# Attention values of a head pair on the two column halves of TensorE, with the softmax sums taken by VectorE

## The chip, the cores and the metric

The kernel runs on one core of one Trainium2 chip. The metric is the device time of one execution in microseconds (us), lower is better. The engines are named as in the profile: PE (TensorE matmul), PEld (its weight loads), DVE (VectorE), ACT (ScalarE), POOL (GpSimd) and SP (SyncE, here the DMA queue).

## The reference

```python
batch, n_heads, seq_l, seq_g, head_dim = (8, 8, 512, 32, 64)
...
s_g = scale * np.matmul(q_g, k_all.transpose(0, 1, 3, 2))
out_g = np.matmul(sm(s_g), v_all)          # 32 global queries see all 544 keys
...
mask = np.abs(pos[:, None] - pos[None, :]) <= 32
s_ll = np.where(mask, s_ll, -1000000000.0) # 512 local queries see a band
s_l = np.concatenate([s_lg, s_ll], axis=-1) # and the 32 global keys
out_l = np.matmul(sm(s_l), np.concatenate([v_g, v_l], axis=2))
...
x = attn_out.transpose(0, 2, 1, 3).reshape(B * S, H * D)
h = x @ w_in                               # 512 -> 2048
g = np.maximum(h, 0.0) + np.log1p(np.exp(-np.abs(h)))
out = g @ w_out                            # 2048 -> 512
```

`sm` subtracts the row's maximum, takes the exponential and divides by the sum plus 1e-9. All data is fp32.

## The kernel before

The work has two parts. Attention runs on pairs of heads: pair m holds two heads, 64 rows of the partitions each, and batch b has the pairs 4b to 4b + 3. The dense layers (the MoE of the code) run per batch in a block of 16 tiles f of 128 hidden columns: 12 passes `h` (input, in a high and a low fp32r half against a weight in two halves) and later 12 passes `o` per f. Blocks 0 to 7 treat the local tokens of one batch, a half block at the end the global tokens of all. In block 0 the weights are also loaded and split into halves, four DVE operations for each of 32 pieces. Batch 0's attention (pairs 0 to 3) runs ahead of everything in code of its own. All other pairs go through `pieces`: small pieces of work with a due number, 12 numbers to a pair, slipped in between the passes of the MoE blocks, which emit the pieces as their own progress `at` moves from `first + 48 * b` to `first + 48 * (b + 1)`; block 0 goes from START = 69 to first + 48.

Each pair is cut into three pieces p of up to 288 queries; a piece has two chunks of 128 keys (32 global keys and 96 local ones). `scores(m, p)` makes scores with keys on the partitions, both heads at once on the two halves of the array's rows (64 rows each), into the PSUM tile "a". For pairs below 8 the mask is added by PE, and ACT copies the scores out; from 8 on DVE adds the mask (L315). L316 is a DVE operation that transposes blocks of 32 x 32 and takes the maximum along the keys, into `mt`. `maxima` folds these partial maxima over the four partition groups (three POOL copies, then short DVE reductions) and spreads them; `probs` spreads them over the keys by a DVE transpose (L347, into `mb`), subtracts on POOL (L352 to L355) and takes the exponential on ACT.

`values(m, p)` multiplies with v. The stationary operand has 65 columns: 64 of v and a column of ones, so that row 64 of the result is the softmax sum. Each head writes its own bank of the PSUM tile "a", partitions 0 to 64. ACT copies the result into `x`, and DVE adds the columns where neighbouring pieces overlap (L374, L375). "a" exists once (two banks), and scores and values share it: every user waits until the one before has been read. `combine`, `invert` and `normalise` take the sums through DRAM: row 64 is written out, read back as 38 x 32, gets 1e-9 and a reciprocal, is written back and read again spread over 64 partitions (`rb`), and two DVE products make the normalised `xa`, head 0 on partitions 0 to 63 and head 1 on 64 to 127. `split_x` makes the fp32r halves `xh` (ACT) and `xl` (DVE) of it for the next block. The 32 global queries stand in all three pieces; the overlap additions sum them too.

PE's order is the order of the code (`mm` chains each matmul to the one before). On the other engines a scheduler sets the order, apart from the dependencies that `after` adds.

Of the kernel before, what the change touches and what calls it, by code (L numbers as in the profile page):

```python
# [53 lines left out]
def moe_over_global_local_attention(  # L54
# [271 lines left out]
    def maxima(m):  # L326
        mt = st.pop(("mt", m))
        for a in range(1, 4):
            nc.gpsimd.tensor_copy(mt[0:32, GW * a:GW * a + GW], mt[32 * a:32 * a + 32, 0:GW])
        e0 = 4 * GW  # L330
        for u, du, off in ((0, 1, -2), (3, 1, 3)):
            nc.vector.tensor_reduce(grid(mt, e0 + u, (7, 6), (du, 2)), grid(mt, 3 + u, (12, 6), (du, 2), (off, 2), (GW, 4)), axis=AX.XY, op=ALU.max)
        nc.vector.tensor_reduce(grid(mt, e0 + 2, (7, 6), (4, 2)), grid(mt, 3 + 2, (12, 6), (7, 2), (GW, 4)), axis=AX.X, op=ALU.max)
# [1 line left out]
        nc.vector.tensor_reduce(grid(mt, g, (1, 2)), grid(mt, 3 + 5, (36, 2), (12, 3), (3, 2), (GW, 4)), axis=AX.XYZ, op=ALU.max)
        nc.vector.tensor_copy(grid(mt, e0 + 5, (21, 2), (7, 3)), mt[0:32, g:g + 2].unsqueeze(2).to_broadcast([32, 2, 3]))
# [6 lines left out]
    def probs(m, p):  # L343
# [12 lines left out]
        nc.scalar.activation(s, s, AF.Exp, scale=0.125)  # L356

    def values(m, p):
        s, vt = st.pop(("s", m, p)), st["v", m]
# [13 lines left out]
        nc.scalar.copy(x[:, :, o + 64:o + w], ps[0:65, :, 64:w])
        nc.vector.tensor_tensor(x[:, :, o:o + 64], x[:, :, o:o + 64], ps[0:65, :, 0:64], op=ALU.add)  # L374
        nc.vector.tensor_tensor(x[:, :, 160:192], x[:, :, 160:192], ps[0:65, :, 160:192], op=ALU.add)  # L375
# [5 lines left out]
    def combine(m):
        nc.sync.dma_start(out=rec_dram[2 * m:2 * m + 2], in_=st["x", m][64:65])

        rows = rec_dram[2 * m:2 * m + 2].rearrange("h (s k) -> (h s) k", k=32)
        sc = pl.tile([38, 32], F32, tag="sc", name=f"sc{m}", bufs=1)
        nc.sync.dma_start(out=sc, in_=rows)
        st["sc", m] = sc, rows

    def invert(m):
# [9 lines left out]
    def normalise(m):  # L399
# [3 lines left out]
        for h in range(2):  # L403
            after(nc.vector.tensor_tensor(y[64 * h:64 * h + 64], x[0:64, h], rb[:, h], op=ALU.mult), "scores")  # L404
# [341 lines left out]
```

## Time and profile before

| | |
|---|---|
| time, median of 3 runs | 1067.12 us (1064.33 to 1071.26) |
| profiled execution, first to last instruction | 1065.3 us |
| PE busy | 1014.5 us (95%), 5108 passes |
| weight loads (PEld) | 804.4 us (76%) |
| DVE | 589.7 us (55%), 1138 instructions |
| ACT | 555.7 us (52%), 998 instructions |
| POOL | 436.9 us (41%), 496 instructions |
| value passes (v_ps) | 672, 114.1 us busy |
| score passes (s_ps) | 672, 78.3 us busy |
| DMA | 75.05 MB, mean 70 GB/s |

The profile is of one execution. Its span is the time from its first to its last instruction; a run's time also holds what lies around that. Busy time is a union over the instructions of a group, "mean ns" the mean duration of one, so with overlap the mean times the count is more than the busy time. In a row of the timeline stand the start, the length, the engine, the line, the operation, its output and inputs, and how often it follows itself; in brackets how long the engine sat idle before, and for whom. A row of the table by stage has the stretch and its length, then for each engine the busy time and the number of instructions, the granted clock of PE, the share of DMA and GB/s.

### The profile page before, as it was taken

To read this page: it belongs to the slowest core of one execution; us is meant where nothing else is said; L and a number is where in the kernel's file an instruction comes from. 1 tells how busy PE (TensorE), PEld (TensorE's weight loads), DVE (VectorE), ACT (ScalarE), POOL (GpSimd) and SP (SyncE) were. 2 spreads that over 40 slices of the span, in tenths; PEclk is the share of its full clock that TensorE was granted. 3 is DMA by queue.
4 is the path that set the end of the run, shared out by engine and by line. 5 is a ranking of instruction groups with operands and counts; after the bars stand their busy time and mean duration, and the time that the engine had idled before them with its cause. 6 is when DMAs were issued, how large, how long until landed. Compare 5 with 4: busy or idle time off the path is not lost.

```text
span 1065.3 us, 14183 instructions
## 1 busy us (share of the span) xinstructions
PE 1014.5 (95%) x5108; PEld 804.4 (76%) x5108; DVE 589.7 (55%) x1138; ACT 555.7 (52%) x998; POOL 436.9 (41%) x496
## 2 busy tenths in 40 slices
PE   7896789889999999999999999999999999999996
...
PEclk9998799999999999999999999999999999999999
...
GB/s 363 171 72 105 100 114 114 95 49 97 46 58 49 94 46 58 47 79 77 57 52 53 97 56 48 55 91 53 48 58 81 54 28 13 73 1 1 14 28 20
DMA packets 78566, 75.05 MB, mean 70 GB/s; under 512 B 53380, under 2 KB 57476, under 8 KB 78496
## 3 DMA queue, kind: packets, MB, share of 16 engines
...
q10 hardware_dynamic: 544, 0.07, 0.0%
...
## 4 chain that ended last, share of the span: by engine, by line
PE 76%; DVE 7%; issue 2%; DMA 2%; POOL 1%; ACT 1%; POOLq 0%; ACTq 0%; DVEq 0%
PE h L126 32%; PE o L126 31%; PE v_ps L126 8%; PE s_ps L126 5%; DMA rb<-rec_scratch 1%; DVE xl L452 1%; DVE xa L404 1%; DVE wbitswo L489 1%; DVE woraw L492 1%; DVE s L315 1%; DMA rec_scratch<-sc 0%; DVE mt L316 0%; DVE wbitswo L486 0%; DVE wbitswi L486 0%; DVE e L543 0%
## 5 line engine op out<-in xcount | busy, mean ns | idle before, releaser
L126 PE MATMUL h<-xh,wi 128*128 128x512 f32 (+1 forms) x1152 | 356.3, 393 | 13.9 <-DVE xl L228 9.2
L126 PE MATMUL o<-wo,gh 128*128 128x512 f32 x1088 | 346.1, 399 | 0.0
L547 POOL TENSOR_TENSOR gl<-e,gh 128x512 fp32r<-128x512 f32 x136 | 176.9, 1300 | 391.1 <-ACT gh L546 315.0
L126 PEld LDWEIGHTS h<-xh,wi 128*128 128x128 f32 x1152 | 209.8, 191 | 59.5 <-issue 14.7
L126 PEld LDWEIGHTS o<-wo,gh 128*128 128x128 f32 x1088 | 200.5, 189 | 45.1 <-issue 5.2
L126 PE MATMUL h<-xl,wi 128*128 128x512 f32 (+1 forms) x576 | 220.4, 383 | 1.3 <-DVE xl L452 1.3
L126 PE MATMUL o<-wo,gl 128*128 128x512 f32 x544 | 213.6, 393 | 0.0
L540 ACT ACTIVATE e<-h 128x512 f32<-128x512 f32 x136 | 81.1, 596 | 239.2 <-PE h L126 239.1
L543 DVE SCALAR_TENSOR_TENSOR e<-h,e 128x512 f32<-128x512 f32 x136 | 93.2, 685 | 173.5 <-ACT e L542 168.5
L352 POOL TENSOR_TENSOR s<-s,mb 128x384 f32<-128x384 f32 x112 | 138.4, 1265 | 14.0 <-DVE mb L347 14.0
L546 ACT CAST gh<-e 128x512 fp32r<-128x512 f32 x136 | 83.9, 617 | 92.4 <-DVE e L543 92.3
L126 PEld LDWEIGHTS h<-xl,wi 128*128 128x128 f32 x576 | 109.4, 190 | 23.8 <-DVE xl L452 1.7
L126 PEld LDWEIGHTS o<-wo,gl 128*128 128x128 f32 x544 | 102.6, 189 | 22.9
L126 PE MATMUL v_ps<-s,v 128*65 128x192 f32 (+1 forms) x672 | 114.1, 313 | 3.8 <-DVE s L315 3.5
L126 PEld LDWEIGHTS v_ps<-s,v 128*65 128x65 f32 x672 | 88.7, 137 | 27.6 <-DVE s L315 5.2
L315 DVE TENSOR_TENSOR s<-s_ps,mask 128x768 f32<-128x768 f32 (+1 forms) x96 | 64.9, 696 | 76.7 <-PE s_ps L126 76.7
L542 ACT ACTIVATE e<-e,one 128x512 f32<-128x512 f32 x136 | 98.4, 723 | 3.1
L126 PE MATMUL s_ps<-raw 64*128 64x192 f32 (+1 forms) x672 | 78.3, 346 | 12.1 <-issue 7.1
L356 ACT ACTIVATE s<-s 128x768 f32<-128x768 f32 (+1 forms) x84 | 66.2, 791 | 41.5 <-POOL s L352 24.4
L541 ACT ACTIVATE e<-e 128x512 f32<-128x512 f32 x136 | 85.7, 630 | 3.6
L126 PEld LDWEIGHTS s_ps<-raw 64*128 64x128 f32 x672 | 53.1, 188 | 43.4 <-issue 30.9
L316 DVE TRANSPOSE_TENSOR_REDUCE mt<-s 128x24 f32<-128x768 f32 (+1 forms) x84 | 76.1, 906 | 10.5 <-ACT s L311 8.7
...
## 6 DMA issues: line engine op xcount, KB each, us to landing
...
```

The lines of the kernel that those rows point to most:

```text
L126: order["pe"] = after(nc.tensor.matmul(*a, **k), "pe").ins
L315: nc.vector.tensor_tensor(s[:, :, o:o + w], ps[:, :, o:o + w], mk.unsqueeze(1).to_broadcast([P, 2, w]), op=ALU.add)
L316: order["scores"] = nc.vector.tensor_reduce(windows(mt, 3 + 12 * p, 36, 2, nb), s.rearrange("p h (b k) -> p h b k", k=32), axis=AX.X, op=A ...
L352: nc.gpsimd.tensor_tensor(sw, sw, windows(mb[:, h], 0, 96, 2, 192), op=ALU.subtract)
L356: nc.scalar.activation(s, s, AF.Exp, scale=0.125)
L404: after(nc.vector.tensor_tensor(y[64 * h:64 * h + 64], x[0:64, h], rb[:, h], op=ALU.mult), "scores")
L540: nc.scalar.activation(e, ph, AF.Abs)
L541: nc.scalar.activation(e, e, AF.Exp, scale=-1.0)
L542: nc.scalar.activation(e, e, AF.Ln, bias=one)
L543: nc.vector.scalar_tensor_tensor(e, ph, 0.0, e, op0=ALU.max, op1=ALU.add)
L546: nc.scalar.copy(gh, e)
L547: nc.gpsimd.tensor_tensor(gl, e, gh.bitcast(F32), op=ALU.subtract)
```

## The change

Values of a pair are now one piece, due at 12 m + 22: for each of the three p and both chunks, head 0 writes partitions 0 to 63 and head 1 partitions 64 to 127 of one PSUM tile, so each uses 64 columns of the array. The pieces lie in the tile at columns 0, 512 and 736; the last two pieces add up in PSUM where they overlap. The ones column is gone. In its place, after the exponential, DVE sums each block over the keys by the same transposing operation as the maxima (L363 of the new file, into `zt`), and `totals`, due at 12 m + 18, folds these sums as the maxima are folded, adds 1e-9, takes the reciprocal and spreads it over 128 partitions by one DVE transpose (`rb`). `normalise` multiplies PSUM by `rb` in three products, then adds the 64 columns of the first overlap and the three copies of the global queries. The copies by ACT, the overlap additions, the DRAM trip and its four DMAs per pair are gone. `first` becomes 61 (from 72), so block 0 covers the due numbers 69 to 109 in place of 69 to 120.

```diff
 QW = (288, 288, 192)
 KWID = (256, 256, 256)
 EW = (0, 544, 1088)
-XOFF = (0, 224, 448)
+OUT = (0, 512, 736)
 NF = DFF // P
 
 M0 = 4
 MPE = 8
-LAG = 22
+VAL = 22
+TOT = 18
 STEP = 3
 GW = 75
 W_AHEAD = 9
...
         st["raw", m, p] = raw
 
     def load_v(m):
-        t = pl.tile([P, 2, 6, 66], F32, tag="v", name=f"v{m}", bufs=2)
-        nc.gpsimd.memset(t[:, :, :, D:D + 1], 1.0)
-        nc.sync.dma_start(out=t[:, :, :, 0:D], in_=v[m - M0].rearrange("p (h c d) -> p h c d", h=2, d=D))
+        t = pl.tile([P, 2, 6, D], F32, tag="v", name=f"v{m}", bufs=2)
+        nc.sync.dma_start(out=t.rearrange("p h c d -> p (h c d)"), in_=v[m - M0])
         st["v", m] = t
 
     def scores(m, p):
...
 
 
 
-    def maxima(m):
-        mt = st.pop(("mt", m))
+    def fold(t, op):
+
         for a in range(1, 4):
+            nc.gpsimd.tensor_copy(t[0:32, GW * a:GW * a + GW], t[32 * a:32 * a + 32, 0:GW])
         e0 = 4 * GW
         for u, du, off in ((0, 1, -2), (3, 1, 3)):
+            nc.vector.tensor_reduce(grid(t, e0 + u, (7, 6), (du, 2)), grid(t, 3 + u, (12, 6), (du, 2), (off, 2), (GW, 4)), axis=AX.XY, op=op)
+        nc.vector.tensor_reduce(grid(t, e0 + 2, (7, 6), (4, 2)), grid(t, 3 + 2, (12, 6), (7, 2), (GW, 4)), axis=AX.X, op=op)
         g = e0 + 44
+        nc.vector.tensor_reduce(grid(t, g, (1, 2)), grid(t, 3 + 5, (36, 2), (12, 3), (3, 2), (GW, 4)), axis=AX.XYZ, op=op)
+        nc.vector.tensor_copy(grid(t, e0 + 5, (21, 2), (7, 3)), t[0:32, g:g + 2].unsqueeze(2).to_broadcast([32, 2, 3]))
+        return t[:, e0:e0 + 44]
+
+    def maxima(m):
+        e = fold(st.pop(("mt", m)), ALU.max)
         for a in range(1, 4):
             i = nc.vector.tensor_copy(e[32 * a:32 * a + 32, 0:42], e[0:32, 0:42]).ins
         order["maxima"] = i
...
             nc.gpsimd.tensor_tensor(s[:, :, 0:192], s[:, :, 0:192], mb[:, :, 0:192], op=ALU.subtract)
             nc.gpsimd.tensor_tensor(s[:, :, 192:288], s[:, :, 192:288], mb[:, :, 96:192], op=ALU.subtract)
         nc.scalar.activation(s, s, AF.Exp, scale=0.125)
-
-    def values(m, p):
-        s, vt = st.pop(("s", m, p)), st["v", m]
-        ps = ps_a.tile([P, 2, 512], F32, tag="a", name=f"v_ps{m}_{p}")
-        parts = ((0, 0, 192), (192, 96, 192 if p < 2 else 96))
-        for h in range(2):
-            for i, (o, qs, w) in enumerate(parts):
-                mm(ps[:65, h, qs:qs + w], lhsT=vt[:, h, 2 * p + i, 0:65], rhs=s[:, h, o:o + w],
-                   start=i == 0, stop=i == 1, skip_group_check=True)
-
         if p == 0:
-            st["x", m] = pl.tile([65, 2, 608], F32, tag="x", name=f"x{m}", bufs=2)
-            nc.scalar.copy(st["x", m][:, :, 0:288], ps[0:65, :, 0:288])
-            return
-        x, o = st["x", m], XOFF[p]
-        w = QW[p] if p < 2 else 160
-        nc.scalar.copy(x[:, :, o + 64:o + w], ps[0:65, :, 64:w])
-        nc.vector.tensor_tensor(x[:, :, o:o + 64], x[:, :, o:o + 64], ps[0:65, :, 0:64], op=ALU.add)
-        nc.vector.tensor_tensor(x[:, :, 160:192], x[:, :, 160:192], ps[0:65, :, 160:192], op=ALU.add)
+            st["zt", m] = pl.tile([P, 348], F32, tag="zt", name=f"zt{m}", bufs=2)
+            nc.gpsimd.memset(windows(st["zt", m], 0, 36, 3, 3), 0.0)
+        nb = 12 if p < 2 else 9
+        nc.vector.tensor_reduce(windows(st["zt", m], 3 + 12 * p, 36, 2, nb), s.rearrange("p h (b k) -> p h b k", k=32),
+                                axis=AX.X, op=ALU.add, apply_transpose=True)
+
+    def totals(m):
+        e = fold(st.pop(("zt", m)), ALU.add)
+        nc.vector.tensor_scalar(e[0:32, 0:42], e[0:32, 0:42], 1e-9, None, op0=ALU.add)
+        nc.vector.reciprocal(e[0:32, 0:42], e[0:32, 0:42])
+        for a in (2, 3, 1):
+            o = 21 * (a // 2)
+            nc.vector.tensor_copy(e[32 * a:32 * a + 32, 0:21], e[0:32, o:o + 21])
+        rb = st["rb", m] = pl.tile([P, 640], F32, tag="rb", name=f"rb{m}", bufs=1)
+        nc.vector.transpose(rb.rearrange("p (s k) -> p s k", k=32), e[:, 0:20].unsqueeze(2).to_broadcast([P, 20, 32]))
+
+    def values(m):
+
+        vt = st["v", m]
+        ps = st["vs", m] = ps_a.tile([P, 2, 512], F32, tag="a", name=f"v_ps{m}")
+        flat = ps.rearrange("p a q -> p (a q)")
+        for p in range(NPC):
+            s = st.pop(("s", m, p))
+            for i, (o, qs, w) in enumerate(((0, 0, 192), (192, 96, 192 if p < 2 else 96))):
+                c = OUT[p] + qs
+                for h in range(2):
+                    mm(flat[64 * h:64 * h + 64, c:c + w], lhsT=vt[:, h, 2 * p + i], rhs=s[:, h, o:o + w],
+                       start=p < 2 and i == 0, stop=True, skip_group_check=True)
 
     xa, ready = {}, set()
 
-    SEG = ((lambda t: t[:, 32:160].unsqueeze(1), 0, 1, 128), (lambda t: windows(t, 192, 224, 2, 192), 128, 2, 192))
-
...
+    SEG = ((lambda t: t[:, 0:128].unsqueeze(1), 0, 1, 128), (lambda t: windows(t, 160, 224, 2, 192), 128, 2, 192))
 
     def normalise(m):
         b, j = divmod(m, H // 2)
-        x, rb = st.pop(("x", m)), st.pop(("rb", m))
+        ps, rb = st.pop(("vs", m)), st.pop(("rb", m))
         y = xa[b, j] = pl.tile([P, 608], F32, tag="xa", name=f"xa{b}_{j}", bufs=4)
-        for h in range(2):
-            after(nc.vector.tensor_tensor(y[64 * h:64 * h + 64], x[0:64, h], rb[:, h], op=ALU.mult), "scores")
-        nc.sync.dma_start(out=xg_dram[j, :, SG * b:SG * b + SG], in_=y[:, 160:192])
+        lap = pl.tile([P, 96], F32, tag="lap", name=f"lap{m}", bufs=2)
+        after(nc.vector.tensor_tensor(y[:, 0:256], ps[:, 0, 32:288], rb[:, 32:288], op=ALU.mult), "scores")
+        nc.vector.tensor_tensor(lap[:, 0:64], ps[:, 1, 0:64], rb[:, 224:288], op=ALU.mult)
+        nc.vector.tensor_tensor(y[:, 256:608], ps[:, 1, 64:416], rb[:, 288:640], op=ALU.mult)
+        nc.vector.tensor_tensor(y[:, 192:256], y[:, 192:256], lap[:, 0:64], op=ALU.add)
+        q = y[:, 128:129]
+        nc.vector.tensor_reduce(lap[:, 64:96], bass.AP(q.tensor, q.offset, [list(q.ap[0]), [1, 32], [224, 3]]), axis=AX.X, op=ALU.add)
+        nc.sync.dma_start(out=xg_dram[j, :, SG * b:SG * b + SG], in_=lap[:, 64:96])
         ready.add((b, j))
-
-    def end(m):
-        return 12 * m + 8 + LAG
 
     def pieces():
         def piece(*fs):
...
                     fs.append(lambda m=m: maxima(m))
                     fs += [lambda m=m, q=q: probs(m, q) for q in range(NPC)]
                 ps.append((12 * m + 4 * p, piece(*fs)))
-                fs = [lambda m=m, p=p: values(m, p)]
-                if p == 2:
-                    fs.append(lambda m=m: combine(m))
-                    if m + 2 < M:
-                        fs.append(lambda m=m: load_v(m + 2))
-                    ps.append((end(m) + STEP, lambda m=m: invert(m)))
-                    ps.append((end(m) + 2 * STEP, lambda m=m: normalise(m)))
-                ps.append((12 * m + 4 * p + LAG, piece(*fs)))
+            ps.append((12 * m + TOT, lambda m=m: totals(m)))
+            fs = [lambda m=m: values(m), lambda m=m: normalise(m)]
+            if m + 2 < M:
+                fs.append(lambda m=m: load_v(m + 2))
+            ps.append((12 * m + VAL, piece(*fs)))
         ps.sort(key=lambda t: t[0])
         return ps
 
...
-    first = end(H // 2 - 1) + 2 * STEP
+    first = 12 * (H // 2 - 1) + VAL + STEP
```

The order of PE's instructions, at the values of pair 14 in block 2 (h2_10 and h2_11 are the input products of the tiles f = 10 and 11 in block 2, o2_0 to o2_3 the output products of its four groups of 128 tokens). Before, the third of three value pieces, each behind other passes:

```order
L126 MATMUL h2_10_3633<-xh2_3_3071,wi11_1255 128x512 x2
L126 MATMUL h2_10_3633<-xl2_3_3072,wi11_1255 128x512
L126 MATMUL v_ps14_2_3655<-s14_2_3227,v14_3196 65x192
L126 MATMUL v_ps14_2_3655<-s14_2_3227,v14_3196 65x96
L126 MATMUL v_ps14_2_3655<-s14_2_3227,v14_3196 65x192
L126 MATMUL v_ps14_2_3655<-s14_2_3227,v14_3196 65x96
L126 MATMUL o2_0_3199<-wo8_1281,gh2_8_3549 128x512 x2
L126 MATMUL o2_0_3199<-wo8_1281,gl2_8_3550 128x512
```

In the changed kernel:

```order
L126 MATMUL h2_11_3703<-xh2_3_3048,wi11_1235 128x512 x2
L126 MATMUL h2_11_3703<-xl2_3_3049,wi11_1235 128x512
L126 MATMUL v_ps14_3725<-s14_0_3298,v14_3270 64x192 x4
L126 MATMUL v_ps14_3725<-s14_1_3357,v14_3270 64x192 x4
L126 MATMUL v_ps14_3725<-s14_2_3428,v14_3270 64x192 x2
L126 MATMUL v_ps14_3725<-s14_2_3428,v14_3270 64x96 x2
L126 MATMUL o2_0_3169<-wo9_1336,gh2_9_3586 128x512 x2
L126 MATMUL o2_0_3169<-wo9_1336,gl2_9_3587 128x512
```

All 12 value matmuls of the pair stand in one stretch, behind the `h` of f = 11 in place of f = 10, with the heads in turn, and 64 output rows in place of 65.

The order of DVE's instructions around the normalising products of pair 14, behind the maxima of a later pair, 16 before and 15 now (mb is the spread maxima, e2_11 the softplus of tile f = 11). Before:

```order
L339 COPY mt16_3562<-mt16_3562 32x42 x3
L347 STREAM_TRANSPOSE mb16_0_3710<-mt16_3562 128x576
L347 STREAM_TRANSPOSE mb16_1_3715<-mt16_3562 128x576
L404 TENSOR_TENSOR xa3_2_3786<-x14_3529,rb14_3743 64x608 x2
L347 STREAM_TRANSPOSE mb16_2_3720<-mt16_3562 128x2x192
L315 TENSOR_TENSOR s17_0_3797<-s_ps17_0_3790,mask_72 128x768
```

In the changed kernel:

```order
L349 STREAM_TRANSPOSE mb15_0_3683<-mt15_3534 128x576
L349 STREAM_TRANSPOSE mb15_1_3691<-mt15_3534 128x576
L398 TENSOR_TENSOR xa3_2_3738<-v_ps14_3725,rb14_3632 128x256
L536 SCALAR_TENSOR_TENSOR e2_11_3716<-h2_11_3703,e2_11_3716 128x512
L399 TENSOR_TENSOR lap14_3739<-v_ps14_3725,rb14_3632 128x64
L400 TENSOR_TENSOR xa3_2_3738<-v_ps14_3725,rb14_3632 128x352
L401 TENSOR_TENSOR xa3_2_3738<-xa3_2_3738,lap14_3739 128x64
L349 STREAM_TRANSPOSE mb15_2_3697<-mt15_3534 128x2x192
L403 TENSOR_REDUCE lap14_3739<-xa3_2_3738 128x32
L363 TENSOR_REDUCE zt15_3688<-s15_0_3536 128x2x12
```

The first product now reads PSUM and stands behind two of the three transposes; the softplus of f = 11 stands between it and the two others, and the sums of pair 15 follow.

The order of DVE's instructions ahead of the first softplus of block 0 (e0_0; wbits, wiraw and woraw belong to the weight splits). Before:

```order
L486 TENSOR_SCALAR wbitswi7_870<-wbitswi7_870 128x512
L488 TENSOR_SCALAR wbitswi7_870<-wbitswi7_870 128x512
L489 SCALAR_TENSOR_TENSOR wbitswi7_870<-wiraw7_162,wbitswi7_870 128x512
L492 SCALAR_TENSOR_TENSOR wiraw7_162<-wiraw7_162,wbitswi7_870 128x512
L486 TENSOR_SCALAR wbitswo4_953<-wbitswo4_953 128x512
L488 TENSOR_SCALAR wbitswo4_953<-wbitswo4_953 128x512
L489 SCALAR_TENSOR_TENSOR wbitswo4_953<-woraw4_164,wbitswo4_953 128x512
L543 SCALAR_TENSOR_TENSOR e0_0_915<-h0_0_902,e0_0_915 128x512
L492 SCALAR_TENSOR_TENSOR woraw4_164<-woraw4_164,wbitswo4_953 128x512
```

In the changed kernel:

```order
L363 TENSOR_REDUCE zt5_862<-s5_1_812 128x2x12
L372 COPY zt4_742<-zt4_742 32x21 x3
L479 TENSOR_SCALAR wbitswi7_893<-wbitswi7_893 128x512
L374 STREAM_TRANSPOSE rb4_830<-zt4_742 128x640
L481 TENSOR_SCALAR wbitswi7_893<-wbitswi7_893 128x512
L363 TENSOR_REDUCE zt5_862<-s5_2_841 128x2x9
L479 TENSOR_SCALAR wbitswo4_992<-wbitswo4_992 128x512
L398 TENSOR_TENSOR xa1_0_960<-v_ps4_947,rb4_830 128x256
L399 TENSOR_TENSOR lap4_961<-v_ps4_947,rb4_830 128x64
L400 TENSOR_TENSOR xa1_0_960<-v_ps4_947,rb4_830 128x352
L482 SCALAR_TENSOR_TENSOR wbitswi7_893<-wiraw7_160,wbitswi7_893 128x512
L536 SCALAR_TENSOR_TENSOR e0_0_938<-h0_0_925,e0_0_938 128x512
```

Sums of pair 5, the spread reciprocals of pair 4 and its three products have moved in ahead of e0_0; part of the weight operations that stood there come behind it.

More of the change, by code (lines that the diff above doesn't have):

```diff
@@ L322, in grid @@
         return bass.AP(base.tensor, base.offset, [list(base.ap[0])] + [list(d) for d in dims])
-    def maxima(m):
-        mt = st.pop(("mt", m))
+    def fold(t, op):
         for a in range(1, 4):
-            nc.gpsimd.tensor_copy(mt[0:32, GW * a:GW * a + GW], mt[32 * a:32 * a + 32, 0:GW])
+            nc.gpsimd.tensor_copy(t[0:32, GW * a:GW * a + GW], t[32 * a:32 * a + 32, 0:GW])
         e0 = 4 * GW
         for u, du, off in ((0, 1, -2), (3, 1, 3)):
-            nc.vector.tensor_reduce(grid(mt, e0 + u, (7, 6), (du, 2)), grid(mt, 3 + u, (12, 6), (du, 2), (off, 2), (GW, 4)), axis=AX.XY, op=ALU.max)
-        nc.vector.tensor_reduce(grid(mt, e0 + 2, (7, 6), (4, 2)), grid(mt, 3 + 2, (12, 6), (7, 2), (GW, 4)), axis=AX.X, op=ALU.max)
+            nc.vector.tensor_reduce(grid(t, e0 + u, (7, 6), (du, 2)), grid(t, 3 + u, (12, 6), (du, 2), (off, 2), (GW, 4)), axis=AX.XY, op=op)
+        nc.vector.tensor_reduce(grid(t, e0 + 2, (7, 6), (4, 2)), grid(t, 3 + 2, (12, 6), (7, 2), (GW, 4)), axis=AX.X, op=op)
         g = e0 + 44
-        nc.vector.tensor_reduce(grid(mt, g, (1, 2)), grid(mt, 3 + 5, (36, 2), (12, 3), (3, 2), (GW, 4)), axis=AX.XYZ, op=ALU.max)
-        nc.vector.tensor_copy(grid(mt, e0 + 5, (21, 2), (7, 3)), mt[0:32, g:g + 2].unsqueeze(2).to_broadcast([32, 2, 3]))
-        e = mt[:, e0:e0 + 44]
+        nc.vector.tensor_reduce(grid(t, g, (1, 2)), grid(t, 3 + 5, (36, 2), (12, 3), (3, 2), (GW, 4)), axis=AX.XYZ, op=op)
[3 more added lines that the diff above has]
+        e = fold(st.pop(("mt", m)), ALU.max)
         for a in range(1, 4):
```

19 lines of the change are left out of this document (1 added, 18 removed).

## The prediction

> **What bounds the kernel now.** I read the busy shares over the span first, then a table by stage, then single PE rows, because the average (PE 95%) hides that the first fifth of the span is another kind of work.
>
> ```profile
> PE   7896789889999999999999999999999999999996
> PEclk9998799999999999999999999999999999999999
> ...
> core 0: us, PE busy (x) PEld busy (x) DVE busy (x) ACT busy (x) POOL busy (x), PEclk, DMA share, GB/s
> 0.00:90.80 90.80, 70.67 (x428) 53.45 (x429) 69.85 (x159) 59.05 (x165) 26.64 (x50) 0.95 0.58 198
> 90.80:242.50 151.70, 131.93 (x620) 99.98 (x621) 124.48 (x203) 85.92 (x147) 89.00 (x85) 0.92 0.29 90
> 242.50:922.00 679.50, 677.46 (x3383) 536.74 (x3382) 372.09 (x744) 344.59 (x581) 290.31 (x339) 1.00 0.22 60
> 922.00:1065.30 143.30, 134.40 (x681) 114.22 (x679) 23.23 (x36) 66.14 (x107) 31.00 (x24) 0.98 0.06 20
> ```
>
> The stages are the start (batch 0's attention), block 0 (90.8 to 242.5, the MoE of batch 0 with the weight splits beside it), blocks 1 to 6 with attention pieces among them, and the tail without attention. From 242.5 to 922 PE is busy 677 of 679.5 us at full clock, DVE 55%, ACT 51%, POOL 43%. So **in that stage the time is the sum of PE's passes**, and a pass taken away there comes off the end. In block 0 it is not: PE waits, its clock is 0.92, and DVE is busy 124 of 152 us.
>
> What a value pass costs on PE is read from where the next rows start (the duration of a row is modelled; starts are not). An fp32 matmul appears as two passes. The first five rows hold one value piece (8 passes of 192 columns on the whole array), the last five one score piece (8 passes of 192 columns, two heads on the two halves of the array's rows).
>
> ```profile
> 617.30 0.62 PE L126 MATMUL h<-xh,wi 128*128 128x512 f32 x2
> 617.75 0.39 PE L126 MATMUL h<-xl,wi 128*128 128x512 f32 x1
> 617.98 1.46 PE L126 MATMUL v_ps<-s,v 128*65 128x192 f32 x8
> 619.14 0.76 PE L126 MATMUL h<-xh,wi 128*128 128x512 f32 x2
> 619.74 0.39 PE L126 MATMUL h<-xl,wi 128*128 128x512 f32 x1
> ...
> 594.12 0.62 PE L126 MATMUL h<-xh,wi 128*128 128x512 f32 x2
> 594.57 0.39 PE L126 MATMUL h<-xl,wi 128*128 128x512 f32 x1
> 594.89 0.92 PE L126 MATMUL s_ps<-raw 64*128 64x192 f32 x8
> 595.74 0.73 PE L126 MATMUL h<-xh,wi 128*128 128x512 f32 x2
> 596.32 0.39 PE L126 MATMUL h<-xl,wi 128*128 128x512 f32 x1
> ```
>
> Two MoE passes take 617.75 - 617.30 = 0.45 us, one takes 0.23. The value piece therefore lasts from 617.98 to 619.74 - 0.45 = 619.29: 1.31 us, 0.164 a pass, with nothing lost on entering or leaving. The score piece would have begun at 594.57 + 0.23 = 594.80 and ends at 596.32 - 0.45 = 595.87: 1.07 us. Eight passes side by side in couples should take half of 1.31, 0.655; the rest, 0.41 us, is what going into the halves and back costs, once per burst.
>
> **The change, part by part.** *Values on PE.* A pair of heads has 20 passes of 192 columns and 4 of 96. Counting the short ones as half, 22 x 0.164 = 3.61 us a pair now. The trace shows no use of the halves of the columns. Nearest is the score piece on the halves of the rows: same dtype, same widths, same two heads in turn. By it a pair would cost 3.61 / 2 + 0.41 = 2.21 us (one burst instead of three), 1.40 less. The bounds: from below no cost of entering, 1.81; from above no couple runs side by side, 3.61 + 0.41 = 4.02. I take 2.21, since the row it comes from differs only in which side of the array is halved.
>
> How many pairs are in the PE-bound stage follows from the passes of each tile:
>
> ```profile
> 90.80:242.50 151.70, 17.83 (x104) 13.66 (x104) 3.27 (x16) 6.49 (x13) 0.92 0.29 90
> 242.50:1065.30 822.80, 96.28 (x568) 74.99 (x568) 19.89 (x96) 34.35 (x71) 1.00 0.19 53
> ...
> 90.80:242.50 151.70, 17.76 (x128) 8.76 (x104) 6.36 (x9) 4.42 (x6) 0.92 0.29 90
> 242.50:1065.30 822.80, 56.98 (x520) 40.70 (x520) 58.58 (x88) 0.00 (x0) 1.00 0.19 53
> ```
>
> The first two rows are v_ps, the last two s_ps. After 242.5 there are 568 / 24 = 23.7 pairs of values and 520 / 24 = 21.7 pairs of scores. In the changed order v8 to v31 stand behind the first pass of block 1, 24 pairs, and scores from s9_1 on, 22.7 pairs: START and `first` let one pair of scores fewer into block 0. So this stage changes by 24 x 2.21 - 23.7 x 3.61 = -32.5 us for values, and by one pair of scores (two pieces of 1.07 and a shorter one, estimated at 0.93 by its four half-length passes) = +3.1 us. **Sum -29.4 us.**
>
> *DVE.* Its rows, and the weight load of a value pass for later:
>
> ```profile
> L126 PEld LDWEIGHTS v_ps<-s,v 128*65 128x65 f32 x672 | 88.7, 137 | 27.6 <-DVE s L315 5.2 <-ACT s L311 0.8
> L404 DVE TENSOR_TENSOR xa<-x,rb 64x608 f32<-64x608 f32 x56 | 68.8, 1229 | 22.1 <-DMA rb<-rec_scratch 21.7
> L316 DVE TRANSPOSE_TENSOR_REDUCE mt<-s 128x24 f32<-128x768 f32 (+1 forms) x84 | 76.1, 906 | 10.5 <-ACT s L311 8.7
> L347 DVE STREAM_TRANSPOSE mb<-mt 128x576 f32<-128x576 f32 (+1 forms) x84 | 56.4, 696 | 1.5
> L374 DVE TENSOR_TENSOR x<-x,v_ps 65x128 f32<-65x128 f32 x56 | 15.8, 283 | 119.1 <-ACT x L373 119.1
> L375 DVE TENSOR_TENSOR x<-x,v_ps 65x64 f32<-65x64 f32 x56 | 11.7, 209 | 0.0
> ```
>
> Removed per pair: two products of 1.23, the lap additions 2 x (0.28 + 0.21), and the small add and reciprocal, 3.9 us. Added: three transposing sums at 0.906 (the maxima's own rows), a fold like that of the maxima (about 1.1 by the rows quoted below), add and reciprocal 0.5, three copies 0.5, one transpose of 640 columns 0.87 (0.696 scaled from a mean of 512), and five operations of normalise over 832 columns in all, about 1.4 by the rate of L374 and L404: 7.1 us. So DVE gains 3.2 us a pair. A pair has about 28.7 us of span (679.5 us hold 23.7 pairs) and 15.7 of DVE; afterwards about 19 of 27.3. PE hides it, with idle time to spare. ACT loses three copies out of PSUM, the SP queue four DMAs a pair, and what stood behind them (raw and weight loads) waits less. POOL loses the ones and gains three short copies and a memset; it is at 43%.
>
> *The new wait.* Values now hold the only "a" tile until normalise's three products on DVE are done; the next scores need it. Behind them in DVE's queue stand further transposes and sums, ahead of them the maxima of the next pair. That chain, as it runs now:
>
> ```profile
> 604.66 0.82 DVE L315 TENSOR_TENSOR s<-s_ps,mask 128x384 f32<-128x384 f32 x2 [2.92 <-PE s_ps L126]
> 605.51 0.78 DVE L316 TRANSPOSE_TENSOR_REDUCE mt<-s 128x18 f32<-128x576 f32 x1
> 607.25 0.54 DVE L332 TENSOR_REDUCE mt<-mt 32x12 f32<-32x96 f32 x2 [0.53 <-POOL mt L329]
> 607.73 0.22 DVE L333 TENSOR_REDUCE mt<-mt 32x12 f32<-32x48 f32 x1
> 607.87 0.22 DVE L335 TENSOR_REDUCE mt<-mt 32x2 f32<-32x48 f32 x1
> 608.35 0.69 DVE L543 SCALAR_TENSOR_TENSOR e<-h,e 128x512 f32<-128x512 f32 x1 [0.26 <-ACT e L542]
> 608.96 0.15 DVE L336 COPY mt<-mt 32x6 f32<-32x6 f32 x1
> 609.14 0.56 DVE L339 COPY mt<-mt 32x42 f32<-32x42 f32 x3
> 609.74 1.44 DVE L347 STREAM_TRANSPOSE mb<-mt 128x576 f32<-128x576 f32 x2
> ```
>
> From 604.66 to the end of the two transposes at 611.18 are 6.5 us, of which 0.95 are an e that the new order has later. Then come the first product (about 0.36), that e (0.69) and two more products (0.65): "a" is free 7.3 us after L315 starts. In the new PE order 12 passes, the value burst and 18 passes lie between those scores and the next: 12 x 0.23 + 2.21 + 18 x 0.23 = 9.1 us. **About 1.8 us of cover**, so I put this wait at nothing in blocks 1 to 6; it is thin, and is a rival below.
>
> *Start and block 0.* Here DVE decides.
>
> ```profile
> 90.81 1.19 PE L126 MATMUL h<-xh,wi 128*128 128x512 f32 x2 [9.22 <-DVE xl L228]
> 102.15 0.69 DVE L543 SCALAR_TENSOR_TENSOR e<-h,e 128x512 f32<-128x512 f32 x1
> 119.31 0.21 DVE L375 TENSOR_TENSOR x<-x,v_ps 65x64 f32<-65x64 f32 x1
> 119.62 1.01 PE L126 MATMUL s_ps<-raw 64*128 64x192 f32 x4 [3.31 <-issue]
> ```
>
> The MoE starts at 90.81, when DVE delivers xl. The sums of pair 4 now come ahead of that xl (three of 0.9, in part in idle time: +1 to +3 us), and the totals of pair 4, sums of pair 5 and a normalise come ahead of the first e, now at 102.15: six to eight us more in front of it. Against this, block 0 has one pair of scores fewer (8 us of DVE by the same rows, and 3.1 of PE), 4 x 1.40 us less of values, and four "a" tiles freed by DVE in place of eight: the wait at 119.62 ends right behind an addition of L375 that stood in DVE's queue, and that addition is gone. Bounds: all of the saved PE work and half of its waits, -14; all of the early delay and nothing back, +10. I take **-3**.
>
> The sum for the profiled execution: 1065.3 - 29.4 - 3 = 1032.9 us. Its span is 1.8 below the median of the runs (1067.1); with that, 1034.7, **1035 us**.
>
> The Trainium skill has a rule against this. "TensorE: Matmul & The Clock Gate", Part 3, says that a weight load overlaps a running matmul only where the two use different row groups; both halves of the columns use all rows. By it a pair would cost 12 x (0.137 + 0.164) + 0.41 = 4.02 us. The trace does not bear that form out: the value passes now use the same rows, their weight loads last 0.137 us, and they still follow each other every 0.164, not every 0.30.
>
> **The rivals.**
> 1. *The halves of the columns don't run side by side* (slower, and the change doesn't do what it says). One couple's second pass waits for the first, or for its weights (0.137 + 0.164 = 0.30 a couple). It decides above (3.61 - 0.41) / 12 = 0.267 us a couple. Serial, a pair costs 4.02: 24 x 4.02 - 23.7 x 3.61 = +10.9, scores +3.1, block 0 about -1: 1080 with the offset. For it: no row shows columns halved. Against it: the score rows, and the hidden weight loads. Chance 0.13.
> 2. *"a" comes free late.* If DVE's chain is over 1.8 us longer than my sum (POOL or ACT late with what it needs), each further us costs one per pair over some 22 pairs. One us late: 1057; half of it 1046. For it: DVE rises from 55% to 70%. Chance 0.16.
> 3. *Block 0 gives nothing back*: +10 in place of -3, 1048; or -14, 1024. These belong to the forecast's own spread.
>
> **How the numbers follow.** Forecast with its spread (1022 to 1048) 0.62; rival 2 beyond that 0.16; rival 1 0.13; better than 1022 0.04; near 1067 by a mixture 0.05. A measurement of this kernel tells about 1% from no change. Faster by over 1% (below 1056): 0.62 + 0.04 + most of rival 2 = 0.78; within 1% 0.08; slower 0.14. The range 1018 to 1064 leaves out rival 1, the rest of the mixture and the far ends.
>
> **What would show it.** PE's value burst: 24 passes within about 2.2 us, two passes in each 0.16 us; the stretch of one pair in blocks 1 to 6 27.3 us in place of 28.7; PE still without idle time there and DVE near 70%; no wait of s_ps on DVE after the value burst; the first MoE pass at 92 to 94 and block 1 at about 240. A burst of about 4 us, or PE waits ahead of s_ps in each pair, would make me wrong, and so would a block 0 that is longer by more than 10 us.

## The result, and the profile after

The changed kernel takes **1028.97 us** (median of 4 runs, 1028.56 to 1030.07) against 1067.84 for the kernel before beside it (1064.33 to 1071.26): ratio 0.9628, 95% interval 0.9607 to 0.9649. The forecast was 1035, with a range of 1018 to 1064. The profiled execution has a span of 1026.8 us, 38.5 less than before.

Where the 38.5 us lie is read from the table by stage, cut at the first MoE pass of block 0 and from there by count, 384 MoE passes to a block, in each kernel. First the kernel before, then the changed one; the columns are the window, its length, busy time and instructions of PE, weight loads, VectorE, ACT and POOL, the granted clock, and the share and GB/s of the DMA.

```profile
0.00:90.81 90.81, 70.67 (x428) 53.46 (x429) 69.86 (x159) 59.06 (x165) 26.64 (x50) 0.95 0.58 198
90.81:241.69 150.88, 131.12 (x616) 99.28 (x617) 123.66 (x202) 85.27 (x146) 88.18 (x84) 0.92 0.29 90
241.69:923.77 682.08, 680.04 (x3393) 538.89 (x3392) 374.19 (x748) 346.42 (x585) 291.12 (x340) 1.00 0.22 60
923.77:1065.30 141.53, 132.63 (x673) 112.75 (x671) 21.94 (x33) 64.95 (x104) 31.00 (x24) 0.98 0.06 20
```

```profile
0.00:91.78 91.78, 67.08 (x429) 51.66 (x429) 74.20 (x163) 59.39 (x165) 27.67 (x53) 0.91 0.54 195
91.78:231.88 140.10, 120.75 (x584) 90.27 (x585) 127.20 (x229) 78.02 (x132) 87.11 (x86) 0.93 0.26 84
231.88:884.23 652.35, 652.35 (x3425) 507.31 (x3424) 463.89 (x1024) 319.19 (x515) 290.07 (x418) 1.00 0.18 52
884.23:1026.80 142.57, 133.62 (x673) 112.38 (x671) 21.55 (x32) 64.93 (x104) 31.00 (x24) 0.98 0.05 18
```

Start +1.0, block 0 **-10.8**, blocks 1 to 6 **-29.7**, tail +1.0: together -38.5. In blocks 1 to 6 PE has no idle time at all now, and VectorE stands at 464 of 652 us, 71%.

The value burst, in the same kind of rows as the value piece before:

```profile
603.05 0.39 PE L126 MATMUL h<-xl,wi 128*128 128x512 f32 x1
603.37 2.01 PE L126 MATMUL v_ps<-s,v 128*64 128x192 f32 x24
605.31 0.74 PE L126 MATMUL o<-wo,gh 128*128 128x512 f32 x2
605.89 0.39 PE L126 MATMUL o<-wo,gl 128*128 128x512 f32 x1
```

Read as in the prediction, the pass ahead ends at 603.05 + 0.23 = 603.28 and the burst ends at 605.89 - 0.45 = 605.44: **2.16 us** for 24 passes (forecast 2.21), where the prediction reckons 3.61 for the three pieces before.

The tile "a" is handed over as follows; VectorE's rows first, then the next scores on PE:

```profile
600.50 0.82 DVE L314 TENSOR_TENSOR s<-s_ps,mask 128x384 f32<-128x384 f32 x2 [0.65 <-PE s_ps L126]
606.12 0.39 DVE L398 TENSOR_TENSOR xa<-v_ps,rb 128x256 f32<-128x256 f32 x1
607.15 0.51 DVE L400 TENSOR_TENSOR xa<-v_ps,rb 128x352 f32<-128x352 f32 x1
```

```profile
609.67 0.92 PE L126 MATMUL s_ps<-raw 64*128 64x192 f32 x8
```

L400 ends at 607.66, 7.16 us after L314 begins (forecast 7.3), and the next scores start at 609.67: 2.0 us of cover (forecast 1.8).

### The profile page after: what moved, and what is told of

It is laid out like the page before. It is cut to its first block, busy times and chain, and to the rows that moved or that the text cites. A ratio compares the mean times of both kernels' runs of the same rounds, so it can differ in the third digit from the quotient of the medians.

```text
span 1026.8 us, 14228 instructions
## 1 busy us (share of the span) xinstructions
PE 973.8 (95%) x5108; PEld 761.6 (74%) x5108; DVE 686.8 (67%) x1446; ACT 521.5 (51%) x914; POOL 435.8 (42%) x580
## 2 busy tenths in 40 slices
DMA packets 34606, 65.93 MB, mean 64 GB/s; under 512 B 7656, under 2 KB 11752, under 8 KB 34536
## 4 chain that ended last, share of the span: by engine, by line
PE 83%; DVE 10%; ACT 2%; POOL 2%; issue 2%; POOLq 0%; ACTq 0%; DVEq 0%
PE o L126 36%; PE h L126 35%; PE s_ps L126 6%; PE v_ps L126 5%; POOL s L354 1%; PE t L126 1%; DVE wiraw L485 1%; DVE wbitswo L479 1%; DVE woraw L485 1%; ACT e L167 1%; DVE wbitswo L482 1%; PE s L126 1%; DVE wbitswo L481 1%; DVE wbitswi L482 1%; DVE mt L315 0%
## 5 line engine op out<-in xcount | busy, mean ns | idle before, releaser
L540 POOL TENSOR_TENSOR gl<-e,gh 128x512 fp32r<-128x512 f32 x136 | 180.0, 1324 | 329.7 <-ACT gh L539 256.4
L536 DVE SCALAR_TENSOR_TENSOR e<-h,e 128x512 f32<-128x512 f32 x136 | 93.2, 685 | 217.1 <-ACT e L535 196.2
L354 POOL TENSOR_TENSOR s<-s,mb 128x384 f32<-128x384 f32 x112 | 113.5, 1042 | 57.8 <-DVE mb L349 57.8
L314 DVE TENSOR_TENSOR s<-s_ps,mask 128x768 f32<-128x768 f32 (+1 forms) x96 | 64.6, 694 | 29.2 <-PE s_ps L126 29.2
L363 DVE TRANSPOSE_TENSOR_REDUCE zt<-s 128x24 f32<-128x768 f32 (+1 forms) x84 | 75.3, 901 | 5.8 <-ACT s L358 4.3
L126 PEld LDWEIGHTS v_ps<-s,v 128*64 128x64 f32 x672 | 45.8, 137 | 17.6 <-issue 9.0
```

Source lines behind the costliest of these rows:

```text
L126: order["pe"] = after(nc.tensor.matmul(*a, **k), "pe").ins
L314: nc.vector.tensor_tensor(s[:, :, o:o + w], ps[:, :, o:o + w], mk.unsqueeze(1).to_broadcast([P, 2, w]), op=ALU.add)
L354: nc.gpsimd.tensor_tensor(sw, sw, windows(mb[:, h], 0, 96, 2, 192), op=ALU.subtract)
L363: nc.vector.tensor_reduce(windows(st["zt", m], 3 + 12 * p, 36, 2, nb), s.rearrange("p h (b k) -> p h b k", k=32), axis=AX.X, op=ALU.add, a ...
L536: nc.vector.scalar_tensor_tensor(e, ph, 0.0, e, op0=ALU.max, op1=ALU.add)
L540: nc.gpsimd.tensor_tensor(gl, e, gh.bitcast(F32), op=ALU.subtract)
```

## Experiments

All start from the changed kernel, called C here, 1028.97 us. The theory is the prediction's: column halves side by side save PE 1.45 us a pair (3.61 - 2.16; forecast 1.40), which comes straight off in blocks 1 to 6. What had to be found out besides is why block 0 gave 10.8 us. Profiles of these kernels reach the first MoE pass at 91.8 in some executions and at 93.5 in others, also where the program up to it is the same as C's, so stages are compared and not single times, and the start's +1.0 us can't be told from nothing.

**e1, the heads one after the other.** Is it the halves side by side, or the one burst, the fewer copies, the missing trip?

```
-        for p in range(NPC):
...
+        for h, p in ((h, p) for h in range(2) for p in range(NPC)):
...
-                for h in range(2):
+                if True:
```

> All twelve value matmuls of head 0 come first, then all of head 1: same burst, same 64-column matmuls, same rest, only no neighbours on different column halves. Theory (the gain is two column halves side by side): the burst lasts 22 x 0.164 + 0.41 = 4.02 us in place of 2.16, so 24 x 1.86 = +45 us in blocks 1 to 6 and 0 to +7 us in block 0 over the changed kernel: 1073 to 1081 us. Rival (the gain comes from one burst in place of three, from fewer ACT copies and from the DRAM trip that is gone): burst and time as in the changed kernel, 1027 to 1032 us.

Measured 1061.78 us, ratio to the kernel before 0.9936 (0.9916 to 0.9956). The burst and blocks 1 to 6 of this kernel:

```profile
622.29 0.39 PE L126 MATMUL h<-xl,wi 128*128 128x512 f32 x1
622.61 3.36 PE L126 MATMUL v_ps<-s,v 128*64 128x192 f32 x24
625.90 0.72 PE L126 MATMUL o<-wo,gh 128*128 128x512 f32 x2
626.47 0.40 PE L126 MATMUL o<-wo,gl 128*128 128x512 f32 x1
```

```profile
93.47:233.63 140.16, 126.01 (x584) 94.87 (x585) 128.29 (x229) 78.25 (x132) 86.39 (x86) 0.94 0.26 84
233.63:918.28 684.65, 684.65 (x3425) 534.44 (x3424) 470.54 (x1024) 318.81 (x515) 289.27 (x418) 1.00 0.17 49
```

The rival falls: with everything else as in C, blocks 1 to 6 lose 32.3 us (684.65 - 652.35), 1.35 a pair of the 1.45 that the burst had saved. The size was expected too high: the burst is 626.47 - 0.45 - 622.52 = 3.50 us, not 4.02. The passes that fall into three equal stretches of it (running over an edge counts too) show why:

```profile
622.90:623.70 0.80, 0.80 (x7) 1.00 0.00 0
623.60:624.40 0.80, 0.80 (x11) 1.00 0.00 0
624.60:625.40 0.80, 0.80 (x8) 1.00 0.00 0
```

In the middle, where head 0 gives way to head 1, 0.8 us holds 11 passes in place of 7 or 8. Two of them are head 0's short ones, of 96 columns; the rest of the surplus are passes of head 1. In the trace a second stream of passes begins at 623.97, while the last pass of the first stream begins only at 624.37: the first passes of head 1 run beside the last of head 0 for about half a us though the program has them behind, and that is nearly all of the 0.52 us. The second lesson is in the first row: PE has 5.3 us more to do in block 0 (126.01 against 120.75), and block 0 is as long as in C (140.16, 140.10). **PE's work does not set block 0.**

**e2, the burst cut in two.**

```
+            ps.append((12 * m + VAL - 0.75, lambda m=m: values(m, 0)))
-            fs = [lambda m=m: values(m), lambda m=m: normalise(m)]
+            fs = [lambda m=m: values(m, 1), lambda m=m: values(m, 2), lambda m=m: normalise(m)]
```

> The values of piece 0 are issued one work item earlier, so that six MoE matmuls stand between them and those of pieces 1 and 2: two bursts in place of one, the tile a held across both. Theory (each burst pays about 0.4 us for entering and leaving the halves): 24 x 0.4 = +9.6 us in blocks 1 to 6 and 0 to +1.6 us in block 0: 1038 to 1041 us. Rival (what looked like a price per burst is the first matmul's wait for its data, or belongs to the number of passes): within 2 us of the changed kernel's 1029.

Measured 1042.84 us, ratio 0.9769 (0.9748 to 0.9790). Blocks 1 to 6:

```profile
233.88:897.05 663.17, 662.65 (x3426) 502.88 (x3424) 462.98 (x1021) 320.74 (x513) 289.32 (x416) 1.00 0.18 51
```

That is 10.8 us more than C for 24 more bursts: 0.45 each (0.5 us of the 10.8 is idle time of PE), where the prediction had taken 0.41 from a score piece. The price is per burst; one burst in place of three on the halves is thus worth about 0.9 us a pair. Block 0 took 142.08 us, 2.0 more than in C, which makes 12.8 of the 13.9 us between the medians.

**e3, block 0 with the pair that the change took out of it.**

```
-    first = 12 * (H // 2 - 1) + VAL + STEP
+    first = 12 * (H // 2 - 1) + VAL + 14
```

> The bound of block 0 goes back from 61 to 72 on the planner's scale, as it was in the kernel before: block 0 takes a pair of scores more and the blocks behind it a pair fewer; values stay as changed. Theory A (PE's work decides block 0): block 0 is 3.1 us longer, blocks 1 to 6 are 3.1 us shorter, the time is that of the changed kernel within 1 us. Theory B (VectorE decides block 0, being busy 91% of it): its about 8 us for that pair come on top, block 0 is 7 to 9 us longer, the rest 3.1 shorter: 1033 to 1035 us.

Measured 1033.40 us, ratio 0.9674 (0.9654 to 0.9694). Block 0 and blocks 1 to 6:

```profile
93.43:242.02 148.59, 124.81 (x633) 93.78 (x633) 139.31 (x265) 79.21 (x134) 89.73 (x97) 0.91 0.28 88
242.02:888.78 646.76, 646.76 (x3377) 503.98 (x3376) 450.12 (x988) 316.66 (x513) 282.44 (x408) 1.00 0.17 50
```

Against C block 0 is 8.5 us longer and the rest 5.6 shorter. The second number shows what I had left out of the expectation: a pair's values move with its scores (2.16 + 3.1 us of PE). Theory B gave the right size in block 0: VectorE has 12.1 us more to do and the block takes 8.5 more. So **in the changed kernel the lower bound is worth 8.5 us in block 0**; 5.6 of them are paid back in later blocks, 1.7 of the difference lie in the start, whose program is the same, and the medians differ by 4.4. The 8.5 can't simply be taken as a part of the 10.8: block 0 of e3 has the 128 score passes of the kernel before, but 120 value passes where that had 104, and five pairs' products where that had four.

**e4, each softmax sum twice.**

```
+        for _ in range(2):
+            nc.vector.tensor_reduce(windows(st["zt", m], 3 + 12 * p, 36, 2, nb), ...
+                                    axis=AX.X, op=ALU.add, apply_transpose=True)
```

> Each transposing sum of the softmax is done twice into the same tile, +2.7 us of VectorE per pair. In blocks 1 to 6 the forecast's view (VectorE is hidden at 70%) gives nothing; the rival there (VectorE is near the bound, or the sums delay the release of a) up to 24 x 2.7 = +65 us. In block 0 and the start, theory B (VectorE decides) gives +10 to +14 us for the five pairs there, theory A (PE decides) 0 to +3. So 1029 to 1043 us by the forecast's view.

Measured 1031.37 us, ratio 0.9652 (0.9631 to 0.9673).

```profile
94.21:236.45 142.24, 123.90 (x584) 92.17 (x585) 132.01 (x238) 77.76 (x131) 80.96 (x84) 0.90 0.26 83
236.45:888.82 652.37, 652.37 (x3425) 507.31 (x3424) 518.76 (x1097) 321.18 (x516) 291.09 (x421) 1.00 0.18 52
```

Blocks 1 to 6 are unchanged to 0.02 us with VectorE at 519 of 652 (80%): its added work really was free there. Block 0 rises by 2.1 us and the start by 2.4, together between theory A's 0 to +3 and theory B's +10 to +14, so this run doesn't decide between them. VectorE's busy time in block 0 rises by 4.8 us only, of which 2.7 fall into its gaps.

**e5 and e6, the tile "a" held longer.** The three products that read "a" are done twice and four times.

```
+        for _ in range(2):          # e6: range(4)
+            after(nc.vector.tensor_tensor(y[:, 0:256], ps[:, 0, 32:288], rb[:, 32:288], op=ALU.mult), "scores")
+            nc.vector.tensor_tensor(lap[:, 0:64], ps[:, 1, 0:64], rb[:, 224:288], op=ALU.mult)
+            nc.vector.tensor_tensor(y[:, 256:608], ps[:, 1, 64:416], rb[:, 288:640], op=ALU.mult)
```

> The three products of normalise that read a are done twice, so the tile a is released 1.1 us later (0.39 + 0.21 + 0.51). Theory (2.0 us of cover between that release and the next scores): blocks 1 to 6 keep their 109.4 us each; block 0 may gain 0 to 4 us. 1028 to 1033 us. Rival (the cover is used up in many pairs): +1.1 us in each, about +26 us.

> The same three products four times: a is released 3.3 us later. Theory: 3.3 - 2.0 = 1.3 us of wait ahead of the next scores in each of 24 pairs of blocks 1 to 6, +31 us, and 0 to +8 us in block 0: 1058 to 1070 us. Rival (VectorE only matters by its total, which goes from 70% to 82%): no wait of scores, 1029 to 1034 us.

Measured: e5 1034.27 us (a little above its range), ratio 0.9687 (0.9674 to 0.9700); e6 **1145.86 us**, ratio 1.0726 (1.0705 to 1.0748). In e5 PE waits little from 233 to 890 us (total, times, longest; the one other wait there is 0.6 us, once):

```profile
PE s_ps L126 <- issue: 3.3, 6, 1.4
```

Six pairs of 24 outlast the cover, and blocks 1 to 6 take 656.93 us, 4.6 more than in C: 2.0 us is right for most pairs, and thin. In e6, from 249 to 1003 us:

```profile
PE s_ps L126 <- issue: 60.9, 22, 3.0
```

The scores now wait in 22 pairs, 2.8 us on average in place of the 1.3 expected, and the loss is larger still (block 0, at 157.40 us, lost 17.3 besides):

```profile
249.21:1003.16 753.95, 693.09 (x3426) 536.80 (x3424) 504.42 (x1228) 321.92 (x513) 285.74 (x415) 0.94 0.15 45
```

Blocks 1 to 6 take 101.6 us more than in C, of which 60.9 are those waits and 40.7 are PE itself, busy 693.09 us for the passes that took 652.35. VectorE's rows explain the waits:

```profile
680.82 0.82 DVE L314 TENSOR_TENSOR s<-s_ps,mask 128x384 f32<-128x384 f32 x2 [0.65 <-PE s_ps L126]
686.44 0.38 DVE L399 TENSOR_TENSOR xa<-v_ps,rb 128x256 f32<-128x256 f32 x1
...
689.72 0.96 DVE L363 TRANSPOSE_TENSOR_REDUCE zt<-s 128x24 f32<-128x768 f32 x1
...
691.48 0.96 DVE L363 TRANSPOSE_TENSOR_REDUCE zt<-s 128x24 f32<-128x768 f32 x1
692.36 0.48 DVE L401 TENSOR_TENSOR xa<-v_ps,rb 128x352 f32<-128x352 f32 x1
```

Two sums and a transpose now stand among the products, and "a" is free at 692.84, 12.0 us after L314 begins: 4.9 beyond C with 2.0 of cover. PE's rows and its granted clock explain the rest:

```profile
692.95 1.25 PE L126 MATMUL s_ps<-raw 64*128 64x192 f32 x8 [2.88 <-issue]
```

```profile
692.95:695.50 2.55, 2.55 (x11) 1.90 (x12) 1.36 (x5) 0.46 (x1) 0.71 (x3) 0.59 0.20 29
695.50:697.00 1.50, 1.50 (x5) 1.15 (x4) 1.50 (x6) 0.00 (x0) 0.00 (x0) 0.56 0.45 159
697.00:700.00 3.00, 3.00 (x15) 2.44 (x14) 2.87 (x8) 1.95 (x3) 0.10 (x1) 1.00 0.00 0
```

After a wait of 2.9 us the granted clock is 0.56 to 0.59 for 4 us, so each us of such waits cost two thirds of a us more (40.7 / 60.9). (The Trainium skill, "TensorE: Matmul & The Clock Gate", Part 1, has the clock halved after an idle window of about 3.4 us; here a wait of 2.9 us, shorter than such a window, was enough.) Rival 2 of the prediction, "a" freed late, is thus a real mechanism with a price above the one it was given; C only stays clear of it.

**e7, the DRAM trip put back**, with nothing on a compute engine reading it: four DMAs a pair, as in `nc.sync.dma_start(out=big, in_=r[:, 0:448].unsqueeze(0).to_broadcast([64, 2, 448]))`.

> The changed kernel with a DRAM trip like the one removed: after each normalise two rows go out, are read back as 38x32, written again and broadcast to 64 partitions (229 KB of the 311 KB before), all on SyncE's queue; no compute engine reads the result. Theory (the DMAs were hidden, the gain is PE's): within 1 us of 1029. Rival (the removed DMAs, 12% of the bytes and over half of the packets, gave part of the gain through SyncE's queue or the memory): 2 to 10 us slower, in block 0 above all, where weights are still loaded.

Measured 1029.95 us, ratio 0.9640 (0.9627 to 0.9653). Blocks 1 to 6 take 652.38 us and block 0 139.78: these DMAs cost nothing. They bring back 6.8 of the 9.1 MB that the change took away (65.93 to 72.77; before 75.05), but only 6400 of its 44,000 packets, so whether the small packets cost anything is not shown. In blocks 1 to 6 of the kernel before PE was idle for 2.0 us in all, so little can have hung on them there.

**e8, masks of two more pairs on PE** (`MPE = 10`).

> Pairs 8 and 9, whose scores fall into block 0 and the start of block 1, get their masks on PE as pairs 4 to 7 do, and ACT instead of VectorE evicts them: VectorE loses about 2 x 2.7 us, PE gains 24 passes of 192 columns, at most 0.164 each, so up to 4 us. Theory B (VectorE decides block 0): 1 to 4 us faster than 1029. Theory A (PE's work decides): 1 to 4 us slower.

Measured 1032.55 us, ratio 0.9668 (0.9654 to 0.9681). VectorE's busy time in block 0 fell by 1.4 us only (125.77), PE's rose by 2.0, and the block took 1.1 more (141.19). The time is 3.6 us above C's, as theory A had it, but 1.7 of that lie in the start and 1.1 in blocks 1 to 6: not a help, and too small a lever to tell A from B.

**e9, VectorE lightened in block 0.** The clamp of the weights' magnitudes is left out there.

```
-        i = nc.vector.tensor_scalar(a.bitcast(F32), a.bitcast(F32), TINY, None, op0=ALU.max)
+        if tight:            # not set behind the start
+            note("dve", nc.vector.tensor_scalar(a.bitcast(F32), a.bitcast(F32), TINY, None, op0=ALU.max))
```

> Left out: the lower clamp of the weights' magnitudes (L479) for the 19 weight tiles that are split in block 0, which takes 13.0 us off VectorE there (12 x 0.746 + 7 x 0.600 in the changed kernel) and nothing off PE, ACT or GpSimd. Block 0 took 140.1 us with VectorE busy 127.2. If VectorE's work decides block 0, it gets 7 to 13 us shorter: 1016 to 1022 us. If PE's work or the chains through ACT and GpSimd do: 0 to 3 us, 1026 to 1029.

Measured 1021.64 us, ratio 0.9567 (0.9543 to 0.9591). Block 0:

```profile
92.39:224.94 132.55, 116.92 (x584) 88.05 (x585) 116.78 (x209) 77.40 (x132) 83.99 (x86) 0.96 0.27 89
```

VectorE has 10.4 us less to do and the block is 7.6 shorter, while 5.3 us of PE's work (e1) moved nothing. **VectorE's work moves block 0, and PE's does not**, at about 0.7 us for each us of VectorE's (8.5 / 12.1 in e3, 7.6 / 10.4 here). That is no fixed price: it is 0.4 in e4 (2.1 / 4.8), and VectorE still has 15.8 us of gaps here.

**e10, e11 and e12, using it.** e10 gives those clamps to GpSimd (`nc.gpsimd.tensor_scalar(...)`); e11 takes one more piece out of block 0 (`first = 12 * (H // 2 - 1) + VAL`); e12 is e10 with the last two tiles of each weight left on VectorE (`if tight or k >= NF - 2`).

> The same 19 clamps on GpSimd, which is busy 87 of 140 us in block 0, in place of VectorE. With VectorE deciding and GpSimd free: up to 13 us shorter, 1016 to 1026 us. If GpSimd's subtractions for gl and for the weights come later by the clamps in their queue (19 of about 1 us): 0 to 10 us slower, 1029 to 1039.

> The bound of block 0 goes from 61 to 58, the lowest at which the first split of batch 1 still finds its pairs done: one piece of scores (of pair 9) less in block 0, 1.07 us of PE and about 1.9 us of VectorE, and the normalise of pair 7 right ahead of the split that reads it. If what a piece costs in block 0 goes on as from 72 to 61 (8.5 us for four pieces): block 0 about 2 us shorter, the rest 1.1 longer: 1028 us. If the split waits for the late normalise: up to 4 us slower.

> As e10, but the clamps of the last two tiles of each weight stay on VectorE. In e10 PE stood 9.7 us ahead of the changed kernel at three quarters of block 0 and gave back 8 at its end, where the last piece of w_out is loaded into the room of the one before only after GpSimd is done with that (211.2 us) and its passes begin at 224.8. If those clamps in GpSimd's queue were what made the end late: 2 to 5 us under e10, 1022 to 1025 us. If the load's wait for its room does: 1026 to 1029 us, no better than e10.

Measured: e10 1027.37 us (0.9615, 0.9594 to 0.9636), no clear gain: with the same clamps taken off it VectorE's busy time in block 0 falls by 1.7 us only (to 125.48), where e9 had 10.4, and GpSimd's rises by 23.8. e11 1041.79 (0.9742, 0.9717 to 0.9768), outside both of its expectations: block 0 falls to 132.06 us, but the blocks behind take 671.11, and PE now waits for the split of each batch, whose pairs are done too late:

```profile
PE h L126 <- DVE xl L445: 8.3, 6, 1.4
PE h L126 <- ACT xh L444: 1.4, 1, 1.4
```

These waits are 9.7 of the 18.8 us lost there. The other 9.1 are PE itself, busy 661.45 us in place of 652.35, of which the moved piece is about one. Four of the waits, 1.4 us each, were followed by a lower granted clock over about 5 us, as in the second row here; after the others it stayed at 1.00. A third of 5 us, four times, is 6.7 us, most of the rest.

```profile
225.50:896.61 671.11, 661.45 (x3430) 510.74 (x3429) 469.39 (x1032) 319.11 (x519) 293.33 (x424) 0.99 0.17 50
452.30:457.30 5.00, 5.00 (x18) 3.67 (x19) 4.09 (x7) 3.42 (x6) 1.41 (x6) 0.66 0.21 56
```

**e12 took 1023.32 us** (1022.89 to 1023.86), ratio 0.9577 (0.9564 to 0.9590), below C's interval: the fastest of the kernels that leave nothing out. Its block 0:

```profile
92.69:226.74 134.05, 119.15 (x585) 89.39 (x586) 123.57 (x215) 76.93 (x130) 104.16 (x97) 0.94 0.27 88
```

By the ranges set for it, the clamps in GpSimd's queue were what made the end of e10 late, not the load's wait for its room. Block 0 is 6.0 us shorter than in C for 3.6 us less of VectorE's busy time, one more sign that busy time there is no fixed price.

## Why the prediction was right, point by point

*Values on PE: right.* 2.16 us a pair against 2.21; e1 shows that the halves side by side earn it, e2 that the fixed price is one per burst (0.45, taken as 0.41). Rival 1 is refuted. By the rule weighed there (the Trainium skill, "TensorE: Matmul & The Clock Gate", Part 3) the burst would have taken 4.02 us; even in e1, where neighbours share rows and columns, 24 passes took 3.50.

*Blocks 1 to 6: right.* -29.7 against -29.4, PE without a wait, a mean of 27.2 us a pair (652.35 / 24; forecast 27.3). That the two agree to 0.3 us is luck: with the measured 2.16 the same sum gives -30.6, and PE's 2.0 us of idle time there (682.08 - 680.04), which the sum left out, are gone as well. About 2.9 us went the other way, and no run shows where.

*VectorE: right where it is hidden.* +97 us in the span (589.65 to 686.84), 3.5 a pair against 3.2. The largest miss among its terms is the small addition:

```profile
L368 DVE TENSOR_SCALAR zt<-zt 32x42 f32<-32x42 f32 x28 | 23.0, 821 | 0.7
L369 DVE RECIPROCAL zt<-zt 32x42 f32<-32x42 f32 x28 | 11.2, 402 | 0.8
```

1.22 us together, where I had put 0.5.

*The new wait: right, and thin.* Cover 2.0 us against 1.8; e5 and e6 bracket it. The price of rival 2, one us for each, was too low: e6 shows 1.7 (101.6 / 60.9).

*Start and block 0: mis-sized.* The step "I take **-3**" measured -9.8 (start +1.0, block 0 -10.8), within its bounds of -14 and +10; it makes the 6 us between 1035 and the time measured. Block 1, put at "about 240" among the signs, began at 231.9. Two of its terms failed. The early delay of "six to eight us" ahead of the first e was small: that e starts at 105.18 in place of 102.15, and the first pass moved by 1.0. And the pair of scores that leaves block 0 was counted as one item among several, where the bound that moves it is worth 8.5 us by e3. Before against e3, with the same score passes and two thirds of a pair of values more, block 0 is 2.3 us shorter: VectorE gets 15.7 us more work (123.66 to 139.31) and loses 17.9 of idle time. What filled that idle time in the kernel before are above all these waits of VectorE in block 0 (the three largest of e3 stand second):

```profile
DVE mt L316 <- ACT s L311: 8.7, 3, 5.4
DVE e L543 <- ACT e L542: 4.8, 3, 2.9
DVE xa L404 <- DMA rb<-rec_scratch: 3.9, 3, 2.7
DVE x L374 <- ACT x L373: 1.3, 2, 1.0
```

```profile
DVE mt L315 <- ACT s L310: 2.5, 1, 2.5
DVE zt L363 <- ACT s L358: 2.3, 2, 1.9
DVE wbitswo L479 <- ACT wbitswo L472: 1.3, 1, 1.3
```

The waits for the broadcast and for the copy into x are gone with those operations, and ACT delivers s earlier. That ACT does so because it has three copies fewer per pair was not tried by itself. The prediction's value for 4 x 1.40 us less of values in block 0 was wrong in kind: in e1 5.3 us of PE's work there were free.

*From span to median:* 2.2 us where 1.8 were taken.
